# A gated attention and a max-out feed-forward on one core: another order of the feed-forward by seven products, and an earlier add of one product

## The chip, the core and the metric

One core of a Trainium2 chip runs the whole kernel in one launch. The metric is the device time of one execution in microseconds (us), lower is better. The engines that matter here are TensorE (PE, matmuls, with its weight loads shown apart as PEld), VectorE (DVE), ScalarE (ACT), GpSimd (POOL) and SyncE (SP, which here issues DMAs only). Each engine runs its own queue in order.

## The reference

```python
# u, v: (8, 3072, 256); z: (8, 3072, 64); scale = 1 / 3072
scores = scale * np.matmul(z, z.transpose(0, 2, 1))
attn = np.maximum(scores, 0.0) ** 2
x = u * np.matmul(attn, v)              # 24576 tokens x 256
h1, h2 = x @ w1, x @ w2                 # w1, w2: 256 x 1024
out = np.maximum(h1, h2) @ w_out        # w_out: 1024 x 256
```

The output is float32. Since max(h1, h2) = relu(h1 - h2) + h2, the kernel computes relu(x @ (w1 - w2)) @ w_out + x @ (w2 @ w_out). `w15_sb` holds w1 - w2 and `W2o_sb` holds w2 @ w_out; both are made once.

## The kernel before

**Work and tiles.** There are 8 batches of 3072 tokens. A batch is 6 groups of 512 tokens, and two neighbouring groups are a couple (c = 0, 1, 2). `A[b, g, blk]` is a block of squared scores, 512 x 512 in bf16. Scores are symmetric, so only the blocks on and above the diagonal are computed; the others are mirrored by DMA transposes that SP issues (L285; parts of the blocks on the diagonal at L267).

**Scores.** `score_pair` makes half a block: two matmuls into two banks of PSUM (L241), two ReLUs on ACT (L254), and later a square, on DVE (L260, L264) or, where `act` is set, on ACT (L262). The pairs are spread over the products of a couple.

**Attention by seven products.** For batches 1 to 7 the product of a couple's 2 x 2 blocks with v is done with seven products instead of eight (P1, P5, P6, P7, X11, X12, X21), on sums and differences of blocks ("forms" S1 to S4, each one DVE instruction over 128 x 2048, L339). `steps_of_couple` gives 84 steps; at each step two matmuls of 64 rows run side by side (L1153). Four accumulator banks, acc0 to acc3, are shared: X12 sums on in P5's bank, X21 in P7's. What a product leaves is taken out by ACT copies (`kept`, L1053) and DVE adds (`add`, L1049). When DVE and ACT do something between the steps is set by `events`, a table by step: the forms S2 of the three block columns stand at steps 22, 26 and 30, the forms S4 at 36, 40 and 44 (`late`), the add of P5 where P5 ends (step 42).

**The feed-forward (ff).** The ff of a couple runs after the products of the couple that follows it. In 14 cases it is `ff_by_seven`, in the other 10 it is `ff`. Of the 8 chunks of 128 hidden units, four are done plainly in each group and four in pairs with seven products. The order of all its work is a string, `FF_ORDER`, read token by token:

- `Nqk`: a plain chunk k of group q, two matmuls of 512 columns (L554) and a ReLU on ACT (L561);
- `P1` to `P7` with x or y: one product, a single matmul of 512 columns (L582). P1, P6, P5, P3 sum on in one bank; after each of the first three ACT copies the sum out (L588, "u"), and P3's sum goes through a ReLU on ACT (L585). P2 sums in a bank of its own; P7 and P4 share one. Each of P2, P7 and P4 ends in a DVE add of a kept sum (L592) and a ReLU of the result (L593);
- `Lqa`, `Lqb`: the linear part x @ W2o, four matmuls of 256 columns (L538);
- `Oqk`: a chunk times w_out, four matmuls of 256 columns (L538);
- `Eq`: the result of a group leaves, two ACT copies (L621) and two DMAs;
- `T`: one task for the next couple, here a form S1 or S3 on DVE (L339).

**Banks.** The sums of scores and of N and P share four banks. `mm_tile` hands them out in turn, past those that a P holds between its first and last sum:

```python
        while True:
            tag = f"mm{bank_turn % 4}"
            bank_turn += 1
            if tag not in held:
                break
```

A new sum waits until whoever reads the old one is done. The order of instructions is the program's order (`manual_schedule`); tiles and semaphores are set by the framework.

Of the kernel before, what the change touches and what calls it, by code (L numbers as in the profile page):

```python
# [11 lines left out]
def kernel(  # L12
# [10 lines left out]
    nc = tc.nc  # L23
    fp32 = mybir.dt.float32
    bf16 = mybir.dt.bfloat16
    AF = mybir.ActivationFunctionType
    ALU = mybir.AluOpType
# [42 lines left out]
    def mm_tile(shape, dtype, name):  # L70
        nonlocal bank_turn
# [5 lines that stand above are left out]
        return mm_psum.tile(shape, dtype, name=name, tag=tag), tag  # L77
# [201 lines left out]
    def mirror_ready(keep=1):  # L279
        while to_mirror and len(free) > keep:  # L280
            mirror(*to_mirror.pop(0))
# [11 lines left out]
    def acc_tile(n):  # L293
        return acc_psum.tile([P, GW], fp32, name=f"acc{n}")
# [171 lines left out]
    def gate(b, g, hs):  # L466
# [13 lines left out]
    FORM_CHUNKS = ((0, KF // 2), (1, KF // 2 + 1))  # L480
    PLAIN_CHUNKS = tuple(n for n in range(KF) if n not in sum(FORM_CHUNKS, ()))
    FF_ORDER = (
        "N03 N00 L1a L0a P1x N02 N01 P1y P6x L0b O02 P2x T N11 O01 P6y P2y O00 P5x P7x O0x1 P5y "
        "L1b P3x O03 P3y P4x O0y1 T N13 O0y2 N12 O11 P7y O1x2 N10 O1x1 T O0x2 P4y O13 E0 O1y2 "
        "O10 T O12 O1y1 E1 T T"
    )

    def weight_forms():
# [15 lines left out]
    def token_forms(b, c):  # L504
        x1, x2 = (xTs[b, q] for q in (2 * c, 2 * c + 1))
        home = Block()
        f = home.ap.rearrange("p (k r) -> p k r", r=GW)
        x_forms[b, c] = home, f
        return [
            lambda: nc.vector.tensor_sub(f[:, 0], x2[:, 0], x2[:, 1]),  # L510
            lambda: nc.vector.tensor_sub(f[:, 1], f[:, 0], x1[:, 0]),
            lambda: nc.vector.tensor_sub(f[:, 2], x1[:, 0], x2[:, 0]),
            lambda: nc.vector.tensor_add(f[:, 3], x1[:, 1], f[:, 1]),
        ]

    def ff_by_seven(b, c, tasks):
# [29 lines left out]
        def new_g(q, name):  # L546
            g_sb[q, name] = gpool.tile([P, GW], bf16, name="g_sb")
            return g_sb[q, name]
# [14 lines left out]
        def part(name, k):  # L563
            n1, n2 = FORM_CHUNKS["xy".index(k)]
            m = "xy".index(k)
            form = lambda n: wT_sb[:, n, ts(m, P)]
            to, w, x = {
                "P1": ("a", w15_sb[:, 0, ts(n1, P)], xs[0][:, 0, :]),
                "P6": ("a", form(1), f[:, 1]),
                "P5": ("a", form(0), f[:, 0]),  # L570
                "P3": ("a", w15_sb[:, 1, ts(n2, P)], f[:, 3]),
                "P2": ("b", w15_sb[:, 1, ts(n1, P)], xs[0][:, 1, :]),
                "P7": ("c", form(2), f[:, 2]),
                "P4": ("c", form(3), xs[1][:, 1, :]),
            }[name]
            first = (k, to) not in acc
            if first:
                acc[k, to], bank[k, to] = mm_tile([P, GW], fp32, "d_ps")
                held.add(bank[k, to])
            ps = acc[k, to]  # L580
            ends = name in ("P3", "P2", "P4")
            nc.tensor.matmul(ps, w, x, start=first, stop=ends, skip_group_check=True)  # L582
            if to == "a":
                if ends:
                    nc.scalar.activation(new_g(0, k + "2"), ps, AF.Relu)  # L585
                else:
                    u_[k, name] = kept[3 * m + ("P1", "P6", "P5").index(name)]
                    nc.scalar.copy(u_[k, name], ps)  # L588
            else:
                q, at, with_ = {"P2": (0, "1", "P1"), "P7": (1, "2", "P5"), "P4": (1, "1", "P6")}[name]  # L590
                g = new_g(q, k + at)
                nc.vector.tensor_add(g, u_[k, with_], ps)  # L592
                nc.vector.tensor_single_scalar(out=g, in_=g, scalar=0.0, op=ALU.max)  # L593
            if ends:
                held.remove(bank[k, to])

# [172 lines left out]
    def emit_pair(wait=0, shared=False, act=False):  # L769
        nonlocal done  # L770
        shared = shared or done < 12 and done % 3 == 0
        finish = score_pair(
            *pairs[done], dve_half=1 if shared else None, halves=done == 0, act=act
        )
        done += 1
        if wait:
            due.append((tick + wait, finish))
        else:
            finish()

    def flush(now=None):
        while due and (now is None or due[0][0] <= now):
            due.pop(0)[1]()
# [29 lines left out]
    with tc.manual_schedule():  # L813
# [55 lines left out]
        for i in range(PLAIN):  # L869
            b, g = groups[i]  # L870
# [5 lines left out]
            for slot, (n, dc) in enumerate(steps_of(i)):  # L876
                k = need(b, g, n)
                upto = max(k, min(done + 1, k + AHEAD)) if slot in slots else k
                while done < min(upto, len(pairs)):
                    emit_pair(  # L880
                        wait=int(i < 2 and slot == slots[-1]), shared=i == 3 and done % 3 == 1
# [96 lines left out]
        def by_seven(i):  # L978
            b, c = couples[i]
            return i + 1 < len(couples) and i >= PLAIN // 2 and c != 1  # L980
# [31 lines left out]
        b, g = groups[PLAIN - 1]  # L1012
# [13 lines left out]
        for i in range(PLAIN // 2, len(couples)):  # L1026
            b, c = couples[i]
# [3 lines left out]
                b, c, forms, blocks=() if b else (q2, q1)  # L1031
# [36 lines left out]
            events = {}  # L1068
            for n, do in enumerate(gates):
                events.setdefault(2 + 3 * n, []).append(do)  # L1070
            if by_seven(i - 1):
                at_forms = {}

                def first_form(i=i):
                    at_forms["do"] = token_forms(*couples[i - 1])
                    at_forms["do"].pop(0)()

                events.setdefault(74, []).append(first_form)
                for n in range(3):
                    events.setdefault(76 + 2 * n, []).append(lambda: at_forms["do"].pop(0)())  # L1080

            def one():
                add(h["1"], h["1"], acc["X11"])
# [4 lines left out]
                add(h["U4"], h["U2"], acc["X12"])  # L1088

            for n, dos in enumerate(late):  # L1090
                for do, steps_in in zip(dos, ((22, 26, 30), (36, 40, 44)) if b else ((24, 30),)):
                    events.setdefault(steps_in[n], []).append(do)
            last = {name: max(ends[name], ends.get("D" + name[1:], 0)) for name in ends}
            for n, do in (
# [39 lines left out]
            for s, pair in enumerate(steps):  # L1134
                tick += 1
                flush(tick)
                mirror_ready()
                for n in at_step.get(s, ()):
                    emit_pair(
                        wait=6, shared=not b and n % 8 == 2, act=b and n in ((0, 6, 8, 10), (0, 1, 6), (0,))[c]  # L1140
                    )
                for do in events.get(s, ()):
                    do()
                for half, (name, w, blk, j) in enumerate(pair):
                    rows = ds(half * R, R)
                    bank = BANK[name]
                    first = bank not in opened
                    if first:
                        opened[bank] = acc_tile(bank)
                    acc[name] = opened[bank]  # L1150
                    a = blk()
                    left[name] -= 1
                    mm = nc.tensor.matmul(  # L1153
                        a.out(acc[name]),
                        w()[rows],
                        a.moving(rows, j),
                        start=first,
                        stop=left[name] == 0,
                        skip_group_check=True,
                    )  # L1160
                    if (s, half) in marks:
                        relay = nc.gpsimd.nop()
                        tc.add_manual_dep(relay.ins, mm.ins.name, AFTER, reason="half done")
                        relays[marks[s, half]] = relay
                    if (s, half) in waits:
                        relay = relays[waits[s, half]]
                        tc.add_manual_dep(mm.ins, relay.ins.name, AFTER, reason="half done")
                    a.quota -= 1
                    if not a.quota:
                        a.release()  # L1170
# [50 lines left out]
```

## Time and profile before

| | |
|---|---|
| median of 3 runs | 914.63 us (912.8 to 914.88) |
| the profiled execution | 914.33 us, span 912.3 us |
| granted PE clock | 0.999 |
| busy: PE, DVE, ACT, POOL | 898.5, 763.8, 678.6, 98.1 us |
| DVE L339, all forms | 260 instructions, 313.0 us |
| DVE L592, adds of the ff by seven | 84 instructions, 57.5 us |
| ACT L588, kept sums of the ff by seven | 84 instructions, 48.2 us |

The times of a part are those of this one profiled execution, from the start of its span. A batch takes 110.8 us from batch 2 on. Matmuls overlap, and their ends are modelled, so the distance from one start to the next tells more than a matmul's length.

### The profile page before, as it was taken

What the parts mean: (1) busy time and instruction counts of PE and PEld (TensorE: products, weight loads), DVE (VectorE), ACT (ScalarE), POOL (GpSimd) and SP (SyncE); (2) the same over time, 40 slices, a digit from 0 to 9 for tenths busy, and PEclk for the clock granted to TensorE, in tenths of its full rate; (3) what the DMA queues carried; (4) which work ended last, traced back from release to release, by engine and by line L of the source; (5) the groups of instructions that cost most, each with busy time, mean ns of one, the idle gap of its engine ahead of it and who ended that gap; (6) DMA issues with size and microseconds to landing.
All of it is one profiled execution on the core that took longest, in us unless ns stands there. A gap on an engine that the chain in (4) does not pass through costs nothing.

```text
span 912.3 us, 19685 instructions
## 1 busy us (share of the span) xinstructions
PE 898.5 (98%) x7448; PEld 520.2 (57%) x7496; DVE 763.8 (84%) x1232; ACT 678.6 (74%) x1273; POOL 98.1 (11%) x176
## 2 busy tenths in 40 slices
PE   9999999999999999999999999999999999999998
PEld 4545656555565555655646556566465564655655
DVE  6897888989888997889978898898988989878842
ACT  7877877777877778777787777876778777784543
POOL 3222100201002010020101101011100110000000
PEclk9999999999999999999999999999999999999999
DMA  9999999989899896999989988899998999797301
GB/s 185 237 221 208 198 199 152 176 159 186 149 198 158 176 175 114 196 162 176 152 145 196 149 177 159 143 166 137 174 198 144 201 152 172 149 138 142 80 24 70
DMA packets 396014, 148.10 MB, mean 162 GB/s; under 512 B 361264, under 2 KB 375856, under 8 KB 395920
## 3 DMA queue, kind: packets, MB, share of 16 engines
q1 hardware_dynamic: 373488, 119.32, 71.0%
q0 software_dynamic: 22288, 27.40, 22.1%
q8 instruction: 58, 0.95, 0.4%
q14 instruction: 36, 0.29, 0.1%
q10 hardware_dynamic: 144, 0.13, 0.0%
HBM read 59.77 MB, written 25.17 MB: 93 GB/s over the span
## 4 chain that ended last, share of the span: by engine, by line
PE 81%; DVE 13%; issue 3%; DMA 2%; ACT 1%; DVEq 0%
PE acc L1153 35%; PE acc L538 11%; PE acc L659 9%; PE d_ps L637 7%; DVE blk L339 6%; PE d_ps L554 5%; PE s_ps L241 5%; PE d_ps L582 4%; PE acc L301 3%; DVE blk L264 3%; DVE xT L469 2%; DMA blk<-blk 1%; DVE h_sb L1049 1%; DVE g_sb L592 0%; ACT r_sb L254 0%
## 5 line engine op out<-in xcount | busy, mean ns | idle before, releaser
L1153 PE MATMUL acc<-blk,v_sb 64*128 64x512 bf16 x2144 | 389.5, 376 | 4.0 <-DVE h_sb L1049 4.0
L254 ACT ACTIVATE r_sb<-s_ps 128x512 bf16<-128x512 f32 (+3 forms) x661 | 328.8, 563 | 66.5 <-PE s_ps L241 29.9
L339 DVE TENSOR_TENSOR blk<-blk,blk 128x2048 bf16<-128x2048 bf16 x260 | 313.0, 1220 | 12.6 <-DMA blk<-blk 9.7
L1153 PE MATMUL acc<-blk,vt 64*128 64x512 bf16 x1560 | 321.4, 376 | 0.0
L1153 PEld LDWEIGHTS <-v_sb 64*128 64x128 bf16 x2144 | 155.2, 94 | 122.8 <-issue 4.9
L264 DVE TENSOR_TENSOR blk<-r_sb 128x1024 bf16<-128x1024 bf16 x201 | 139.2, 706 | 51.5 <-ACT r_sb L254 50.2
L1153 PEld LDWEIGHTS <-vt 64*128 64x128 bf16 x1560 | 126.2, 94 | 78.9 <-issue 10.7
L241 PE MATMUL s_ps<-zT 64*128 64x512 bf16 (+3 forms) x672 | 137.6, 358 | 0.9 <-DVE r_sb L252 0.7
L538 PE MATMUL acc<-w_out_sb,g_sb 128*128 128x256 bf16 x896 | 123.0, 273 | 0.8
L650 ACT ACTIVATE g_sb<-d_ps 128x512 bf16<-128x512 f32 x152 | 88.3, 601 | 47.4 <-PE d_ps L637 40.5
L538 PEld LDWEIGHTS <-g_sb 128*128 128x128 bf16 x896 | 87.6, 98 | 35.6
L561 ACT ACTIVATE g_sb<-d_ps 128x512 bf16<-128x512 f32 x112 | 63.9, 598 | 42.4 <-PE d_ps L554 21.4
L659 PE MATMUL acc<-w_out_sb,g_sb 128*128 128x256 bf16 x632 | 93.3, 273 | 0.0
L637 PE MATMUL d_ps<-xT,w_sb 128*128 128x512 bf16 x300 | 89.2, 379 | 1.2 <-issue 0.2
L592 DVE TENSOR_TENSOR g_sb<-blk,d_ps 128x512 bf16<-128x512 f32 x84 | 57.5, 684 | 32.5 <-PE d_ps L582 32.5
L659 PEld LDWEIGHTS <-g_sb 128*128 128x128 bf16 x632 | 61.8, 98 | 34.9
L183 POOL DMA_DIRECT2D v_sb<-in_v_dram x90 | 48.0, 551 | 237.6 <-PE acc L1153 226.3
L469 DVE SCALAR_TENSOR_TENSOR xT<-h_sb,uT 128x512 bf16<-128x512 f32 x96 | 60.7, 689 | 3.5 <-PE d_ps L637 3.5
L1049 DVE TENSOR_TENSOR h_sb<-h_sb,acc 128x512 f32<-128x512 f32 x89 | 58.7, 681 | 5.8 <-PE acc L1153 5.8
L241 PEld LDWEIGHTS <-zT 64*128 64x128 bf16 x672 | 41.1, 94 | 35.9 <-issue 0.4
L554 PE MATMUL d_ps<-xT,w_sb 128*128 128x512 bf16 x196 | 58.4, 380 | 1.2
L588 ACT COPY blk<-d_ps 128x512 f32<-128x512 f32 x84 | 48.2, 597 | 14.8 <-PE d_ps L582 14.0
(89 smaller groups left out, 733.6 us busy)
## 6 DMA issues: line engine op xcount, KB each, us to landing
out_dram<-o_sb SPq DMA_DIRECT2D x95, 256.0 KB, 2.8
un<-in_u_dram POOLq DMA_DIRECT2D x44, 256.0 KB, 5.7
v_sb<-in_v_dram POOLq DMA_DIRECT2D x84, 128.0 KB, 6.6
blk<-blk SPq DMA_TRANSPOSE x240, 4.7
zn<-in_z_dram POOLq DMA_DIRECT2D x18, 128.0 KB, 4.5
blk<-in_u_dram SPq DMA_DIRECT2D x4, 512.0 KB, 4.5
v_sb<-in_v_dram POOLq DMA_DIRECT2D x6, 256.0 KB, 6.1
blk<-in_moe_w_dram SPq DMA_DIRECT2D x2, 512.0 KB, 4.4
```

Source lines behind the costliest of these rows:

```text
L241: nc.tensor.matmul(s_ps[h][:, lo[h] :], zT[rows, z_at(b, blk * G + tiles[h], h), :], zT[rows, q + lo[h] // P : q + G, :].rearrange("p t c ...
L254: nc.scalar.activation(o, s, AF.Relu)
L264: nc.vector.tensor_mul(a[:, k : k + 2, :], r, r)
L339: op(*((by_key(x) if mixed else x.ap) for x in blocks))
L469: lambda dc=dc: nc.vector.scalar_tensor_tensor(out=x[:, dc, :].rearrange("p (t r) -> p t r", r=P), in0=hs[dc].rearrange("p (t r) -> p t r" ...
L538: nc.tensor.matmul(o_ps[key][:, t % 2, :], x[:, ts(t, P)], w, start=first, stop=stop and t % 2 == 1,)
L554: nc.tensor.matmul(d_ps, w15_sb[:, kc, ts(nb, P)], xs[q][:, kc, :], start=kc == 0, stop=kc == KD - 1,)
L637: nc.tensor.matmul(d_ps, w15_sb[:, kc, ts(nb, P)], xs[q][:, kc, :], start=(kc == 0), stop=(kc == KD - 1),)
L650: nc.scalar.activation(g_sb[q, nb], d_ps, AF.Relu)
L659: nc.tensor.matmul(o_ps[key][:, t % 2, :], x[:, ts(t, P)], w, start=first, stop=ends and (t % 2 == 1 or len(tiles) == 1) and n == len(weig ...
L1049: nc.vector.tensor_add(out, a, b_)
L1153: mm = nc.tensor.matmul(a.out(acc[name]), w()[rows], a.moving(rows, j), start=first, stop=left[name] == 0, skip_group_check=True,)
```

## The change

It does five things:

- `FF_ORDER` is another string. The same tokens are in it; three of the six T stand ahead of the first sum that DVE adds to (P7x), and P7x comes before P2y, P4x, P7y, P2x and P4y.
- The ReLU of the six added sums of each ff by seven (L593) goes from DVE to ACT, in place.
- The forms S4 stand at steps 36, 44 and 48 instead of 36, 40 and 44. The add of P5 stays at step 42.
- The four differences of the tokens (`token_forms`) stand at steps 70, 71, 72 and 73 instead of 74, 76, 78 and 80.
- The squares that ACT does: in couples c = 1 those of pairs 0, 6, 7 instead of 0, 1, 6; in couples c = 2 those of pairs 3 and 6 instead of 0.

```diff
     FF_ORDER = (
-        "N03 N00 L1a L0a P1x N02 N01 P1y P6x L0b O02 P2x T N11 O01 P6y P2y O00 P5x P7x O0x1 P5y "
-        "L1b P3x O03 P3y P4x O0y1 T N13 O0y2 N12 O11 P7y O1x2 N10 O1x1 T O0x2 P4y O13 E0 O1y2 "
-        "O10 T O12 O1y1 E1 T T"
+        "N02 T P1x T N11 L0a N00 L1a P1y P6x N13 N12 L0b T O00 P5x L1b N01 N10 O02 P6y N03 "
+        "O11 P7x O01 P5y P3x P2y O13 P4x O10 O03 P3y P7y O0x2 P2x O1x2 P4y O0y1 O1x1 O0y2 "
+        "O0x1 T E0 O1y1 O12 T O1y2 E1 T"
     )
...
                 nc.vector.tensor_add(g, u_[k, with_], ps)
-                nc.vector.tensor_single_scalar(out=g, in_=g, scalar=0.0, op=ALU.max)
+                nc.scalar.activation(g, g, AF.Relu)
...
-                events.setdefault(74, []).append(first_form)
+                events.setdefault(70, []).append(first_form)
                 for n in range(3):
-                    events.setdefault(76 + 2 * n, []).append(lambda: at_forms["do"].pop(0)())
+                    events.setdefault(71 + n, []).append(lambda: at_forms["do"].pop(0)())
...
-                for do, steps_in in zip(dos, ((22, 26, 30), (36, 40, 44)) if b else ((24, 30),)):
+                for do, steps_in in zip(dos, ((22, 26, 30), (36, 44, 48)) if b else ((24, 30),)):
...
-                        wait=6, shared=not b and n % 8 == 2, act=b and n in ((0, 6, 8, 10), (0, 1, 6), (0,))[c]
+                        wait=6, shared=not b and n % 8 == 2, act=b and n in ((0, 6, 8, 10), (0, 6, 7), (3, 6))[c]
```

## The prediction

> **What bounds the kernel now.** I read the page's busy times first, then the waits of PE, then the stretches of a period, last the timeline around each wait.
>
> ```profile
> PE 898.5 (98%) x7448; PEld 520.2 (57%) x7496; DVE 763.8 (84%) x1232; ACT 678.6 (74%) x1273; POOL 98.1 (11%) x176
> PE acc L1153 <- DVE h_sb L1049: 4.0, 13, 1.3
> ```
>
> PE has work in 98% of the span, so time is won or lost only where PE's stream of matmuls has a hole. The second line (PE's waits: total us, times, longest) is nearly all the holes in the steady part: 13 waits of products (L1153) for the add on DVE at L1049. The same list shows no wait inside the ff by seven, but it leaves out short ones, so I looked at the stretches.
>
> ```profile
> 291.08:306.59 15.51, 15.37 (x110) 10.68 (x112) 12.50 (x21) 10.16 (x19) 0.00 (x0) 1.00 0.81 134
> 269.82:291.08 21.26, 20.99 (x197) 11.23 (x197) 19.86 (x39) 17.41 (x36) 5.83 (x11) 1.00 1.01 182
> 306.59:328.40 21.81, 21.62 (x197) 9.95 (x197) 20.77 (x28) 17.98 (x34) 1.77 (x4) 1.00 1.01 200
> ```
>
> Columns: stretch, its length, then busy time (instructions) of PE, PEld, DVE, ACT, POOL, granted clock, DMA. First an ff by seven, then the products of a couple c=1 and of one c=2. All 14 ffs by seven last 15.5 us. In the ff ACT is busy 10.2 of 15.5, so its mean has room; in the products DVE is busy 19.9 of 21.3 and 20.8 of 21.8: it lags there. The holes, in the timeline (start, duration, what, and in brackets the idle time and who ended it):
>
> ```profile
> 299.10 1.25 ACT L585 ACTIVATE g_sb<-d_ps 128x512 bf16<-128x512 f32 x2
> 299.34 0.38 PE L582 MATMUL d_ps<-blk,w_sb 128*128 128x512 bf16 x1
> 299.55 0.38 PE L582 MATMUL d_ps<-xT,wT_sb 128*128 128x512 bf16 x1
> 299.77 0.60 PE L538 MATMUL acc<-w_out_sb,g_sb 128*128 128x256 bf16 x4
> 299.97 0.69 DVE L592 TENSOR_TENSOR g_sb<-blk,d_ps 128x512 bf16<-128x512 f32 x1 [0.27 <-PE d_ps L582]
> 300.40 0.38 PE L554 MATMUL d_ps<-xT,w_sb 128*128 128x512 bf16 x1
> ```
>
> The matmul at 299.34 is P3y; its ReLU is the second of the two at 299.10 (it ends at 300.35). N13 gets the bank that P3y leaves: due at 300.21 (299.77 and four matmuls of 0.109), it starts at 300.40. So a bank is free for the next sum at the earliest 1.06 us after its last matmul started, and the ff's one hole is 0.19 us.
>
> ```profile
> 281.94 1.22 DVE L339 TENSOR_TENSOR blk<-blk,blk 128x2048 bf16<-128x2048 bf16 x1
> 283.08 0.68 DVE L1049 TENSOR_TENSOR h_sb<-h_sb,acc 128x512 f32<-128x512 f32 x1
> 283.17 0.38 PE L1153 MATMUL acc<-blk,vt 64*128 64x512 bf16 x1
> 283.81 0.37 PE L1153 MATMUL acc<-blk,v_sb 64*128 64x512 bf16 x1 [0.27 <-DVE h_sb L1049]
> ```
>
> X12 sums on in P5's bank, so its first matmul waits for the add of P5. That add stands behind the form at 281.94. Starts are 0.64 apart where 0.21 is usual: 0.43 lost. The same place of a c=2 (320.41 to 320.97) loses 0.35, and that of the first couple of batch 1 (134.47 to 136.12) 1.43.
>
> **The add of P5.** The built order on DVE puts it ahead of one more form (S4 of the second block, step 40 to 44); the third form, 44 to 48, stood behind it already. So it passes one, and a form holds DVE 1.13 us (starts 281.94 and 283.08). In c=1 the add would end near 282.6 where X12 is due at 283.38. In c=2 it passes a form too, and X12 was due at 320.62 against an end of 320.92: the hole goes. The 1.43 becomes 0.3. What is late next are the two S4 forms: in c=1 the second would end at 283.8 (X12 reaches that block four steps, about 0.95 us, after its start: 284.3), the third at 284.9 (due 285.2). They hold, with 0.3 us at the tightest. Sum: 6 x 0.43 + 6 x 0.35 + 1.1 = **5.8 us gained**. One square in c=1 changes places between DVE and ACT, one in c=2 goes from DVE to ACT (L262, 1.06 us, of an engine with 3.8 us free): it only helps DVE. The four token forms come 4 to 7 steps earlier; their inputs are the ff's xT of a couple before: nothing.
>
> **The new order of the ff.** PE does the same matmuls. I walked it with rows: 0.216 us a matmul of 512 columns, 0.109 one of 256 (N 0.432, P 0.216, O and L 0.436); a sum's drain starts on ACT 0.41 after the matmul's start (299.34 to 299.75) and on DVE 0.42 to 0.49, taken 0.45; ACT's drain lasts 0.60 and the next starts 0.49 later; an add (L592) 0.69; the next engine starts 0.05 to 0.1 after an end. The old order so walked has one hole, N13, 0.20 us: measured 0.19. So I trust the walk.
>
> The new one, from the ff's start. Eight N, five P, four L and three O come before P7x: 3.46 + 1.08 + 1.74 + 1.31 = 7.59. Then O01, P5y at 8.24, P3x at 8.46, P2y due at 8.67. The new banks go round in turn, past those held, and P2y's is the one that P3x has just left: the built program makes P2y wait for P3x's ReLU on ACT. Where the old order has a P4 and an O between, this has nothing: even with ACT free the hole is 1.06 - 0.22 = 0.84 us (0.86 by the walk's own slots).
>
> And ACT isn't free. Its queue there is: ReLU of P7x, copy of P5y, ReLU of P3x. The first is the moved one, and waits for DVE: sum at 7.59, add 8.04 to 8.73, ReLU from 8.83. Then the copy at 9.31, P3x's ReLU at 9.80 to 10.40, P2y at 10.45: a hole of **1.78 us**. Behind the waiting ReLU stand just these two, and PE waits for the second. The moved ReLU's time isn't in the trace: the nearest rows are ACT's 512 elements out of PSUM (0.60, next start 0.49) and L262's 1024 in SBUF (1.06, less than twice that): I take 0.58 and 0.48; half of L262 (0.53) and 0.60 bound it, some 0.1 us either way.
>
> The rest of the walk has no hole. The tightest are P4y (sum at 13.70; P7y's add frees its bank at 13.59) and O1y1 (15.67; P4y's ReLU is ready at 15.58); with every hand-over 0.1 later they would cost up to 0.2 an ff. The three forms (T) ahead of the first sum run on DVE at about 2.5 to 5.9, before the first add at 8.04; the transposes that the three read had landed before the ff's start (the latest at 362.3, for the ff at 365.1). Each ff so grows by 1.78 - 0.20 = 1.58: 14 x 1.58 = **22.1 us lost**. DVE gives up 6 ReLUs of 0.21 (the old L593, 0.29 with its tail), but it isn't late there.
>
> The Trainium skill, "ScalarE: Activation LUTs", Rules for kernel authors, speaks against the move: relu belongs on VectorE, which it calls up to about 3 times as fast per element in bf16. With three times L593's 0.29, 0.88, in the place of 0.48, the hole would be 2.18 and the time about 5.6 us longer; no row here shows that form, and L262 speaks for the smaller figure.
>
> **Sum.** The profiled execution took 914.33 us (span 912.3 and 2.0 around it), 0.3 under the median of the runs. 914.33 + 22.1 - 5.8 = **930.6 us**. PE has nothing else to wait for, so the holes add up in full; a longer one does not slow what follows (after the 1.43 at 136.12 starts are 0.21 apart again).
>
> **Rivals.**
> - ACT gets through its queue early (P7x's add or ReLU much shorter than the rows), and only the bare hand-over of 0.86 is left: 14 x (0.86 - 0.20) = 9.2, less 5.8: 917.7. Against it: three instructions in a row with known rows. 0.07.
> - Faster: P3x's drain is hidden after all, and both old holes go: 914.33 - 14 x 0.19 - 5.8 = 905.9. It decides once P2y's hole is under 0.19 + 5.8 / 14 = 0.60 us. For it: one bank is free then (N03's, drained at 8.0). Against: the turn skips it, and 0.86 is the floor that N13 shows. 0.04.
> - The early add gains nothing, as it passes one form, and S4 or the square before it ends late instead: 914.33 + 22.1 = 936.4. Against: the margins of 0.3 us and more above. 0.08.
> - ACT's end is late as well, and P4y and O1y1 wait 0.2 an ff: 933.4. 0.11, inside the range.
>
> **How the numbers follow.** The forecast itself has 0.70. Its own errors: 0.1 us in the hand-overs x 14 is 1.4, in the ReLU's two slots the same, the gain 2: about 927 to 934. The range reaches up to the late add, nearly, and down half way to the first rival: 922 to 936. Within 0.3% (2.7 us, about what a measurement can tell here) of the time before lies only the low end of the first rival: same 0.03. Faster 0.04. Slower 0.93.
>
> **What would show it.** In the profile after: each ff by seven 17.1 us instead of 15.5; one wait in each, of PE at L582 for ACT L585, 1.6 to 1.9 us (an idle time of some 1.4 to 1.7 after the modelled end of a matmul), just behind an ACT L593; no wait at N13 (L554); the 13 waits for DVE L1049 gone, or only the first left with 0.1 to 0.3; ACT some 40 us busier (84 x 0.5), DVE 18 to 25 less. It is wrong if the ff stays under 16.2 us, or if new waits stand in the products.

## The result and the profile after

The changed kernel takes 926.34 us (median of 5, 925.88 to 929.52) and the kernel before, beside it, 912.80 (median of 5, 911.86 to 914.88): ratio 1.0149 (95% interval 1.0127 to 1.0172), 13.5 us slower. The profiled execution after took 929.52 us, span 927.5.

First the page's busy times and the longest of PE's waits (total us, times, longest):

```profile
PE 892.6 (96%) x7448; PEld 509.6 (55%) x7496; DVE 742.5 (80%) x1143; ACT 727.4 (78%) x1362; POOL 96.7 (10%) x176
PE d_ps L582 <- ACT g_sb L585: 24.6, 14, 1.8
```

The 13 waits of products for the add at L1049 are gone from the list. In their place stand 14 waits of one kind, one in each ff by seven: a product (L582) for the ReLU of P3 (L585). The stretches that answer to the three of before:

```profile
295.09:312.11 17.02, 15.21 (x112) 10.66 (x112) 12.13 (x15) 13.33 (x25) 0.00 (x0) 1.00 1.00 147
274.47:295.09 20.62, 20.62 (x198) 10.61 (x197) 18.98 (x39) 17.36 (x36) 5.82 (x11) 1.00 1.00 167
312.11:333.36 21.25, 21.25 (x197) 9.47 (x197) 18.71 (x26) 18.91 (x35) 1.58 (x4) 1.00 0.99 196
```

The ff is 1.51 us longer (15.51 to 17.02), the products of a c=1 are 0.64 shorter and those of a c=2 0.56; in both, PE is now busy from end to end. Then the place of the new wait in the timeline:

```profile
302.69 0.38 PE L582 MATMUL d_ps<-blk,wT_sb 128*128 128x512 bf16 x1
303.11 0.69 DVE L592 TENSOR_TENSOR g_sb<-blk,d_ps 128x512 bf16<-128x512 f32 x1 [2.07 <-PE d_ps L582]
303.34 0.38 PE L582 MATMUL d_ps<-blk,wT_sb 128*128 128x512 bf16 x1
303.82 0.63 ACT L593 ACTIVATE g_sb<-g_sb 128x512 bf16<-128x512 bf16 x1 [0.72 <-DVE g_sb L592]
304.36 0.57 ACT L588 COPY blk<-d_ps 128x512 f32<-128x512 f32 x1
304.82 0.60 ACT L585 ACTIVATE g_sb<-d_ps 128x512 bf16<-128x512 f32 x1
305.48 0.38 PE L582 MATMUL d_ps<-xT,w_sb 128*128 128x512 bf16 x1 [1.76 <-ACT g_sb L585]
```

The matmuls are P7x, P5y and P2y; P3x, due at 303.56, has no record in this trace. P2y was due at 303.34 + 2 x 0.216 = 303.77 and starts at 305.48: a hole of 1.71 us. ScalarE's queue reads as forecast: the ReLU of P7x waits for DVE's add, the copy of P5y and the ReLU of P3x stand behind it.

**Where the time went.** From the start of batch 1's first couple to the end the trace before takes 791.3 us and the one after 803.8, 12.5 more: 14 x 1.51 = 21.1 lost in the ffs; gained are 6 x 0.64 in the c=1, 6 x 0.55 in the c=2 and 0.04 in the last c=1, 7.2 together, and 1.4 in the first couple of batch 1 (22.58 to 21.20). The rest between the two profiles, 2.7 us, lies ahead of batch 1, where no instruction has changed. That part ends between 120.4 and 123.7 us in the ten profiles of this study, so below I compare parts rather than single times.

The 1.4 can't be put down to the change. The same couple takes 20.94 us in experiment 6, where no instruction up to its end differs from the kernel before, and 22.77 in experiment 4, where none differs from the changed kernel. Its length goes with how far DVE lags when it starts. The first line below is from the kernel before, where the couple starts at 120.97, the second from experiment 6, where it starts at 122.71:

```profile
123.62 0.28 DVE L494 TENSOR_TENSOR wT_sb<-w_sb 128x256 bf16<-128x256 bf16 x1
123.36 0.29 DVE L494 TENSOR_TENSOR wT_sb<-w_sb 128x256 bf16<-128x256 bf16 x1
```

DVE comes to this instruction 2.65 us after the couple's start in the kernel before, 0.65 in experiment 6, 2.09 in the changed kernel and 3.66 in experiment 4; where it is under 1.4, in seven of the ten profiles, the couple takes 20.94 to 21.04. Why the lag differs from profile to profile is open. Without this couple the change costs 21.1 - 7.2 = 13.9 us, near the 13.5 of the medians.

### The profile page after: what moved, and what is told of

The parts are those of the page before. It is cut to its first block, busy times and chain, and to the rows that moved or that the text cites. A ratio compares the mean times of both kernels' runs of the same rounds, so it can differ in the third digit from the quotient of the medians.

```text
span 927.5 us, 19629 instructions
## 1 busy us (share of the span) xinstructions
PE 892.6 (96%) x7448; PEld 509.6 (55%) x7496; DVE 742.5 (80%) x1143; ACT 727.4 (78%) x1362; POOL 96.7 (10%) x176
## 4 chain that ended last, share of the span: by engine, by line
PE 93%; DVE 3%; ACT 3%; DMA 0%; issue 0%; DVEq 0%
PE acc L1153 43%; PE acc L538 13%; PE acc L659 9%; PE d_ps L637 7%; PE s_ps L241 7%; PE d_ps L554 5%; PE d_ps L582 4%; PE acc L301 4%; DVE g_sb L592 1%; ACT g_sb L593 1%; ACT g_sb L585 1%; ACT blk L588 1%; DVE blk L264 1%; DMA blk<-blk 0%; DVE blk L339 0%
## 5 line engine op out<-in xcount | busy, mean ns | idle before, releaser
L1153 PE MATMUL acc<-blk,vt 64*128 64x512 bf16 x1560 | 318.1, 377 | 0.0
L1153 PEld LDWEIGHTS <-v_sb 64*128 64x128 bf16 x2144 | 152.9, 94 | 125.9 <-issue 6.0
L264 DVE TENSOR_TENSOR blk<-r_sb 128x1024 bf16<-128x1024 bf16 x196 | 134.7, 699 | 55.0 <-ACT r_sb L254 54.0
L241 PE MATMUL s_ps<-zT 64*128 64x512 bf16 (+3 forms) x672 | 129.2, 359 | 2.4 <-DVE r_sb L252 2.3
L538 PE MATMUL acc<-w_out_sb,g_sb 128*128 128x256 bf16 x896 | 118.4, 273 | 0.0
L592 DVE TENSOR_TENSOR g_sb<-blk,d_ps 128x512 bf16<-128x512 f32 x84 | 55.5, 686 | 65.2 <-PE d_ps L582 55.5
L659 PE MATMUL acc<-w_out_sb,g_sb 128*128 128x256 bf16 x632 | 93.4, 273 | 0.0
L593 ACT ACTIVATE g_sb<-g_sb 128x512 bf16<-128x512 bf16 x84 | 52.4, 630 | 30.9 <-DVE g_sb L592 30.3
L1049 DVE TENSOR_TENSOR h_sb<-h_sb,acc 128x512 f32<-128x512 f32 x89 | 58.6, 680 | 7.1 <-PE acc L1153 6.7
L262 ACT ACTIVATE blk<-r_sb 128x1024 bf16<-128x1024 bf16 x59 | 62.5, 1059 | 1.3
```

Source lines behind the costliest of these rows:

```text
L241: nc.tensor.matmul(s_ps[h][:, lo[h] :], zT[rows, z_at(b, blk * G + tiles[h], h), :], zT[rows, q + lo[h] // P : q + G, :].rearrange("p t c ...
L264: nc.vector.tensor_mul(a[:, k : k + 2, :], r, r)
L538: nc.tensor.matmul(o_ps[key][:, t % 2, :], x[:, ts(t, P)], w, start=first, stop=stop and t % 2 == 1,)
L659: nc.tensor.matmul(o_ps[key][:, t % 2, :], x[:, ts(t, P)], w, start=first, stop=ends and (t % 2 == 1 or len(tiles) == 1) and n == len(weig ...
L1153: mm = nc.tensor.matmul(a.out(acc[name]), w()[rows], a.moving(rows, j), start=first, stop=left[name] == 0, skip_group_check=True,)
```

## The experiments

Times are medians; beside the first four the kernel before took 912.85 us, beside the others 912.68. "Rest" is the profile's time from the start of batch 1's first couple, with that couple in it.

| kernel | ff by seven | c=1 | c=2 | rest | time | ratio to before (95%) |
|---|---|---|---|---|---|---|
| before | 15.51 | 21.26 | 21.81 | 791.3 | 912.7 to 912.9 | 1 |
| after | 17.02 | 20.62 | 21.26 | 803.8 | 926.34 | 1.0149 (1.0127 to 1.0172) |
| P2y in another bank | 15.93 | 20.62 | 21.26 | 788.6 | 911.71 | 0.9982 (0.9972 to 0.9993) |
| P2y and P2x in other banks | 15.31 | 20.62 | 21.26 | 779.9 | 902.91 | 0.9881 (0.9856 to 0.9905) |
| before, S4 later | 15.51 | 20.62 | 21.60 | 784.5 | 909.37 | 0.9946 (0.9925 to 0.9967) |
| after, all six ReLUs on DVE | 16.58 | 20.62 | 21.26 | 799.3 | 921.75 | 1.0088 (1.0061 to 1.0116) |
| after, S4 back | 17.02 | 20.63 | 21.26 | 804.1 | 927.60 | 1.0170 (1.0147 to 1.0193) |
| before, ReLUs on ScalarE | 17.33 | 21.35 | 21.75 | 815.8 | 940.19 | 1.0305 (1.0285 to 1.0326) |
| after, P7x's ReLU on DVE | 16.43 | 20.62 | 21.26 | 795.9 | 918.49 | 1.0067 (1.0047 to 1.0088) |
| before, all but the ff | 15.51 | 20.62 | 21.26 | 782.5 | 905.86 | 0.9933 (0.9918 to 0.9948) |

**1. P2y in another bank.** The changed kernel; the turn of the banks is moved on by two ahead of P2y.

```diff
         def part(name, k):
+            nonlocal bank_turn
...
             if first:
+                bank_turn += {'P2y': 2}.get(name + k, 0)
                 acc[k, to], bank[k, to] = mm_tile([P, GW], fp32, "d_ps")
```

> The changed kernel with one thing else: P2y takes the bank that N03 has left, two further in the turn, and not the one that P3x has just left. No instruction moves. Theory (the hole is the hand-over of P3x's bank): P2y's hole of 1.71 us goes; by the same walk P2x then meets a bank that P3y has just left and waits 0.66, so an ff by seven takes 17.02 - 1.06 = 15.96 us and the whole some 14.8 us less than the changed kernel, near 911.5. Rival (ScalarE is simply too full with six more ReLUs, wherever the bank lies): the ff stays near 17.0 and the whole near 926.

Measured: ff 15.93 us, 911.71 us. P2y's hole is gone; PE's waits name the one that was to follow, P2x's, 0.62 us by the starts (two lines were added above it, so L584 and L587 are L582 and L585 of the changed kernel):

```profile
PE d_ps L584 <- ACT g_sb L587: 6.4, 14, 0.5
```

ScalarE's busy time in an ff is the same 13.3 us as in the changed kernel, and its queue starts with the same ReLU. It isn't its load, then, but who waits for its queue.

**2. Two banks.** As in the first, and one further for P2x.

```diff
-                bank_turn += {'P2y': 2}.get(name + k, 0)
+                bank_turn += {'P2y': 2, 'P2x': 1}.get(name + k, 0)
```

> As the one before, and P2x too takes another bank, one further in the turn. Theory: no hole is left in the ff by seven by the walk, 15.30 us each; 14 x 1.72 = 24.1 us less than the changed kernel, near 902. That would be under the kernel before too. Rival (ScalarE too full): the ff stays above 16.5 us, the whole above 919.

Measured: 902.91 us, under both kernels, by 1.2% under the one before. The stretch of an ff of this kernel, and the longest of PE's waits that are left, at 86 us and so ahead of batch 1:

```profile
250.76:266.07 15.31, 15.21 (x110) 10.68 (x110) 12.45 (x16) 13.28 (x26) 1.06 (x2) 1.00 1.09 191
PE s_ps L241 <- DVE r_sb L252: 1.7, 1, 1.7
```

No wait is left in an ff by seven. The order and ScalarE's ReLUs are all those of the changed kernel: its whole loss hung on the banks of two products.

**3. The add of P5 alone.** The kernel before, S4 later.

```diff
-                for do, steps_in in zip(dos, ((22, 26, 30), (36, 40, 44)) if b else ((24, 30),)):
+                for do, steps_in in zip(dos, ((22, 26, 30), (36, 44, 48)) if b else ((24, 30),)):
```

> The kernel before with the steps 36, 44, 48 for the forms S4 and nothing else. Theory (the gain between the ffs is the add of P5 passing one form): the ffs stay at 15.51 us, the 13 waits of products for the add go, and the products' stretches come out as in the changed kernel (20.62 for c=1, 21.26 for c=2): 8.5 us less than before, near 904.5. By the size that the prediction gave those holes it would be 5.8 less, near 907. Rival (DVE's relief in the changed ff, or the squares moved, gave that gain): less than half of it, and holes of 0.3 us or more stay in the products.

Measured: 6.8 us less in the rest (791.3 to 784.5), 3.5 by the medians of whole runs; the part ahead of batch 1 ended at 123.1 in this profile against 121.0 before. Of the 6.8, 1.6 lie in the first couple of batch 1 (22.58 to 20.94) and are not shown to be the edit's; 5.1 are. All 13 waits for the add are gone and a c=1 is as short as in the changed kernel, but a c=2 keeps 0.34. DVE and PE there, in the timeline:

```profile
318.09 0.68 DVE L1049 TENSOR_TENSOR h_sb<-h_sb,acc 128x512 f32<-128x512 f32 x1
318.69 0.68 DVE L264 TENSOR_TENSOR blk<-r_sb 128x1024 bf16<-128x1024 bf16 x1
319.29 2.35 DVE L339 TENSOR_TENSOR blk<-blk,blk 128x2048 bf16<-128x2048 bf16 x2
320.26 0.38 PE L1153 MATMUL acc<-blk,vt 64*128 64x512 bf16 x1
320.56 0.37 PE L1153 MATMUL acc<-blk,v_sb 64*128 64x512 bf16 x1
320.56 0.39 PE L1153 MATMUL acc<-blk,vt 64*128 64x512 bf16 x1
```

Behind the add of P5 (L1049) stands a square (L264), and then the two forms, S4 of the second and third block (319.29 and 320.43). X12 reaches the second block at 320.26 and its form ends at 320.51: what the prediction named as late next is late here.

**4. All six ReLUs on DVE.** The changed kernel with the old line L593.

```diff
-                nc.scalar.activation(g, g, AF.Relu)
+                nc.vector.tensor_single_scalar(out=g, in_=g, scalar=0.0, op=ALU.max)
```

> The changed kernel with its six ReLUs of sums back on DVE. Theory (hand-over of the bank plus ScalarE's queue): the queue's part goes with the ReLU, the hand-over stays: P2y waits 1.13 us and not 1.71, another 0.08 comes at O1y1, the ff takes 16.5 us, the whole 7 us less than the changed kernel, near 919. If the ReLU on ScalarE were all of the loss, the ff would be at 15.3 to 15.5 and the whole near 904; if it had no part, 17.0 and 926.

Measured: 921.75 us, and an ff of 16.58 us, so 0.44 less, near the 16.5 expected:

```profile
257.36:273.94 16.58, 15.35 (x110) 10.58 (x111) 13.32 (x22) 10.00 (x20) 1.06 (x2) 1.00 1.10 187
```

The new order loses 1.1 us an ff with no ReLU moved at all: P2y waits 1.12 and O1y1, for the ReLU of P4y on DVE, 0.14. By the medians the kernel is 4.6 us faster than the changed one, not 7: the ffs give 14 x 0.44 = 6.2, and in the profiles the first couple of batch 1 takes 1.6 back (22.77 us against 21.20), with no edited instruction ahead of its end.

**5. S4 back.** The changed kernel with steps 36, 40, 44.

> The changed kernel with the forms S4 back at steps 36, 40 and 44, so that the add of P5 stands behind the second form again. In the changed kernel's trace that add ends 1.18 us before X12's start in a c=1 and about 1.5 before it in a c=2; a form holds DVE 1.13. Theory (the add's place and DVE's relief each close the holes, and either would do): holes of 0 to 0.1 us only in c=1 and c=2, ffs 17.02, and the time within 1.5 us of the changed kernel. Rival (it is the add's place alone that closes them): c=1 back at 21.2, c=2 at 21.8, 8 us more, near 934.

Measured: c=1 20.63, c=2 21.26, 927.60 us. In the changed kernel the earlier add is worth next to nothing, as DVE is less behind there: in a c=1 the add starts 12.63 us after the couple's start here, 13.26 in the kernel before. Which of the other parts makes DVE earlier (the forms' earlier places in the ff, the squares, the token forms) is not separated. The moved ReLUs alone don't: in experiment 6 the add starts at 13.33.

**6. The ReLUs alone.** The kernel before with L593 on ScalarE, its own order.

> The kernel before with nothing changed but the six ReLUs of sums, on ScalarE. By the walk with the measured rows (ReLU 0.63 on ScalarE, next start 0.54 later, 0.02 after the add) the old order would have four holes: 0.14 at P7x, 0.43 at P3x, 1.24 at P3y, 0.20 at N13, so an ff of 17.3 us and a time 25 us over the kernel before, near 938, less what DVE's relief closes of the 13 holes in the products (up to 8.5, if it closes them all). If the ReLU's engine alone cost nothing and the order were all: ff 15.5 and 905 to 913.

Measured: ff 17.33 us (17.31 by the walk), 940.19 us, and the waits that the walk named:

```profile
PE d_ps L582 <- ACT blk L588: 18.2, 28, 1.0
```

28 waits of products for kept sums, two in each ff, at P3x and P3y: there the moved ReLU holds up the copies behind it. The holes of the products stay (c=1 21.35, c=2 21.75), so DVE's relief from these ReLUs doesn't close them.

**7. One ReLU back.** The changed kernel, P7x's ReLU on DVE.

```diff
-                nc.scalar.activation(g, g, AF.Relu)
+                if name + k == "P7x":
+                    nc.vector.tensor_single_scalar(out=g, in_=g, scalar=0.0, op=ALU.max)
+                else:
+                    nc.scalar.activation(g, g, AF.Relu)
```

> The changed kernel with the ReLU of one sum, P7x's, back on DVE (two of the twelve products' ends in x and y; the other five ReLUs of an ff stay on ScalarE). Theory (of P2y's 1.71 us the hand-over of the bank is one part and that one ReLU in ScalarE's queue the other): P2y waits 1.13, the ff takes 16.43 us, 14 x 0.59 = 8 us less than the changed kernel, near 918, as with all six ReLUs on DVE or a little better. Rival (the load of all six counts): the ff stays above 16.8.

Measured: ff 16.43 us, 918.49 us, both as expected. ("Two of the twelve" there should read one of the six.) The same place in its timeline:

```profile
261.20 0.38 PE L582 MATMUL d_ps<-blk,w_sb 128*128 128x512 bf16 x1
261.40 0.59 ACT L588 COPY blk<-d_ps 128x512 f32<-128x512 f32 x1 [0.65 <-PE d_ps L582]
261.88 0.60 ACT L585 ACTIVATE g_sb<-d_ps 128x512 bf16<-128x512 f32 x1
262.54 0.38 PE L582 MATMUL d_ps<-xT,w_sb 128*128 128x512 bf16 x1 [0.96 <-ACT g_sb L585]
```

P3x at 261.20, P2y due at 261.42 and started at 262.54: 1.12. So of the 1.71 the one ReLU makes 0.59, and 1.12 is the bank's hand-over with the copy of P5y ahead of P3x's ReLU.

**8. All but the ff.** The kernel before with S4, token forms and squares as changed.

> The kernel before with every part of the change outside the ff by seven: S4 at 36, 44, 48, the token forms at 70 to 73, the other squares on ScalarE. With S4 alone a c=2 still lost 0.34 us at X12's waits for the second and third S4 form. Theory (DVE was late there, the square moved to ScalarE frees 0.6 of it): c=2 comes down from 21.60 to 21.3, c=1 stays at 20.62, ffs at 15.51: about 2 us under the kernel with S4 alone. Rival (that rest needs the lighter ff): c=2 stays at 21.6 and the time is that of S4 alone.

Measured: c=2 21.26, rest 782.5, 2.0 under the third experiment; 905.86 us. The add of P5 and what follows it on DVE, in a c=2:

```profile
315.50 0.69 DVE L1049 TENSOR_TENSOR h_sb<-h_sb,acc 128x512 f32<-128x512 f32 x1
316.09 2.36 DVE L339 TENSOR_TENSOR blk<-blk,blk 128x2048 bf16<-128x2048 bf16 x2
```

The add starts 12.51 us after the couple's start, as in the third experiment, but the square that stood between it and the two S4 forms is gone, and they come 0.6 us earlier: in time. Outside the ff the change is worth 7.2 us in the c=1 and c=2, as much as the changed kernel gains there; the 8.8 of the rest have the 1.6 of the first couple in them.

## Why the prediction was right

**P2y's hole** was forecast as 1.78 us and is 1.71. The mechanism came as forecast, step by step; two of its terms were off the most, and they nearly cancel. The hand-over from the add to the ReLU was taken as 0.1 us, from ScalarE's waits for DVE, and is 0.03 (303.79 to 303.82, before the rows are rounded). The ReLU holds ScalarE 0.54 and lasts 0.63 (0.48 and 0.58 were taken, and half of L262 with 0.60 as the bounds: it lies just above); ScalarE is 48.8 us busier in the page, where some 40 were forecast. The add's start and the copy's slot were 0.03 shorter each. The ff comes to 17.02 where 17.09 was forecast: 21.1 us lost, not 22.1.

**Its two parts** are shown separately: without P7x's ReLU in ScalarE's queue 0.59 goes (experiment 7), and with another bank all of it (experiment 1). The first rival, a queue that ScalarE gets through early, falls by the timeline; the faster one was two banks away, and experiment 2 is what it looks like. With P2y's bank alone its condition, a hole of P2y under 0.60, is met, but P2x's new wait of 0.62 takes its place, and the kernel is only 0.2% under the one before (experiment 1).

**The add of P5** was put at 5.8 us: 4.7 in the c=1 and c=2, where the changed kernel gains 7.2, and 1.1 in the first couple of batch 1, where no run shows a gain that is the change's. The step that was mis-sized is the hole itself. I took 0.21 us off the distance of 0.64 as the usual one, but X12's first matmul has a partner on the other 64 rows and is due with it: without the wait the two start together, as the changed kernel shows at the same place.

```profile
287.81 0.38 PE L1153 MATMUL acc<-blk,vt 64*128 64x512 bf16 x1
287.82 0.38 PE L1153 MATMUL acc<-blk,v_sb 64*128 64x512 bf16 x1
```

So a c=1 had lost 0.64 and a c=2 0.56: just what they came down by. The reason was half the story: the earlier add closes the holes by itself (experiment 3), save 0.34 in a c=2, and the other parts of the change close them without it (experiment 5). That the gain came at the changed kernel is thus no proof of the reason given for it. The prediction called the moved squares a help to DVE and gave them nothing; beside the earlier add, in the kernel before, they are worth the 2.0 us of experiment 8.

**The third rival** (the add gains nothing) fails as to the time, and in the kernel before the add gains by itself; its mechanism, the S4 forms late, exists: 0.34 us in a c=2 of experiment 3. In the changed kernel the add does gain next to nothing, but as the holes are closed without it (experiment 5). **The fourth** (P4y and O1y1 late as well) did not come: the trace after has no wait there. The sum by measured parts is 21.1 - 7.2 = 13.9 where 16.3 was forecast; 930.6 is further off, as it starts from 914.33 and the kernel before took 912.80 beside the changed one.

**The rule on relu.** The Trainium skill ("ScalarE: Activation LUTs", Rules for kernel authors) gives relu to VectorE, up to about 3 times as fast per element in bf16. Measured on the same tile: 0.63 us on ScalarE against 0.29 on DVE, 2.1 times, within that. What the move costs hangs on who waits behind it: 1.82 us an ff in the old order (experiment 6), 0.44 in the new one (experiment 4). With both banks changed the ReLUs stay on ScalarE, no wait is left in the ff, and the kernel is the fastest of all; that kernel with the ReLUs on DVE was not run.

## What to carry to other kernels

Where buffers go round in turn, an order of work is only half a schedule: walk through which buffer each new sum gets, and who reads it last. An engine with a fifth of its time free can still cost the bound engine, if a wait stands ahead of a drain in its queue. And of two matmuls that run side by side, a wait of one costs its whole length: compare it with its partner, not with the one before.

## What the runs showed of the hardware

A wait of ScalarE for DVE ended 0.03 us after the add here (42 waits), against 0.09 for its ReLUs of scores that wait for a square of DVE. The 14 holes of 1.71 us changed neither the granted clock (1.00 in that stretch) nor the pace after them (0.22 a matmul of 512 columns).
